# Two layers of attention and feed-forward on one core: new clocks for the program that writes the order of the instructions

## The chip, the cores and the metric

The kernel runs on one core of a Trainium2 chip. The metric is the device time of one execution in microseconds. Three executions of the kernel before took 1618.16, 1618.6 and 1620.25 us (median 1618.6 us); a further one was profiled. The core's engines are TensorE (PE, with its weight loads PEld), VectorE (DVE), ScalarE (ACT), GpSimd (POOL) and SyncE (SP), which issues most DMAs. Each engine works through its own list of instructions in order, and waits on semaphores for what others produce.

## The reference

The input `x` has 2048 rows of 512 (bfloat16). Two equal layers follow each other:

```
x = x + attention(layernorm(x), wqkv, wo)     # 32 heads of 16 columns
x = x + silu(layernorm(x) @ w1) @ w2          # 512 -> 1792 -> 512
```

Attention is `softmax(q k^T / 4) v` over all 2048 keys, so each layer has 32 x 2048 x 2048 exponentials. The result has the shape and type of `x`.

## The kernel before

*Tiles.* Queries are taken in four chunks of 512 rows (`NQC`), heads in eight groups of four (`HB`). One chunk and one group make a segment (`Seg`); there are 74, because some of layer 1's are split into "old" keys (rows 0 to 1535) and "new" keys, so that layer 1 can start before layer 0's last chunk is through its feed-forward. A segment goes over its keys in blocks of 128; a score tile is one key block with two of the four heads, 128 x 1024 numbers in PSUM. There are 2048 score tiles and three PSUM buffers for them (`slot`).

*Scores (L1282).* Two matmuls of 32 rows make a tile. A further row of each head's query carries a bound on the scores, so that no maximum has to be taken. This is the work of `q_pieces`: it loads the raw query `qc` from DRAM (L240), takes its absolute value `qu` (L404), multiplies the keys' maxima `amax` into a small matrix `bm` (L412), forms a product of the two on TensorE (`q_bias`, below "the bias product", tile `q_ps`), and adds it to the query (L421) to make `QT`, the tile that scores read. In the first chunk of layer 0 (segments 0 and 2 to 8) the keys and their maxima are made one segment ahead as well: `k_piece` (matmuls, copy L334, `KT` L321), `amax_piece` (L348) and `amax_all` (L355).

*Exponentials.* Most tiles go to ScalarE (L1503). The others go to VectorE, which writes a bfloat16 bit pattern straight from the scores (L1537); three further terms of the same tile are made by adding constants to the bits, on GpSimd (L1598) or, if the queue of them gets long, on VectorE (L1571). Such a tile has four rows to be multiplied with V instead of one.

*Values (L1358).* Each row is multiplied with V and a column of ones, accumulating in `o_ps`, one bank of PSUM. When a segment's rows are through, `close` copies `o_ps` to `oT` (L1184, L1180 or L1176). A DMA transposes it to `at`; a reciprocal (L513) and a product (L514), both in `heads_norm`, give `attn`.

*The rest.* A chunk's epilogue (`epilogue_pieces`) transposes `attn` by DMA into the buffer `hT`, of which there is one, multiplies with `wo`, and adds to `x`. `ffn_pieces` does the layer norm (L227), the first product with a tanh on ScalarE (L580), L584, and the second product (L593). `next_pieces` does layer 1's norm and V rows (`v_piece`, L379).

*The order.* Nothing is scheduled at run time. The class `Flow` plays the kernel through with a clock for each engine (`self.pe`, `self.act`, `self.dve`, `self.pool`, `self.sp`) and writes each engine's list on the way. `run` lets the engine with the earliest clock take a turn. `pe_turn` chooses between scores of the next tile or two, values whose rows are ready (`fit`), a step of a side piece (`head`: keys, queries, feed-forward), and a fill-in product that nothing reads (`warm`, L1398), which is allowed only while little has run lately. `act_turn` and `dve_turn` and `pool_turn` do the same for theirs. The order is thus as good as the clocks: what each instruction takes, when its result may be read, when a buffer comes free (`slot_free`), and when the port that VectorE and GpSimd share is taken (`lock` by a GpSimd shift, `held_port` by a VectorE operation marked `"l"`).

Before, an operation's end serves both as the time when its engine can go on and, with 50 ns more, as the time when others may read the result:

```
end = self.dve = at + ns
lat = (50, 0, 50)
```

The order does not know when a query tile will be there: `pe_turn` writes the next segment's scores as soon as the step that makes `QT` has been written and a slot is free. The same holds for V rows (`v_made`) and for the buffer `hT`.

*Letters.* Every 16 tiles (`STRETCH`) a letter of `RULES` picks seven settings from `KINDS`: how many spare buffers and how short a queue of shifts are required before VectorE may take a tile, when waiting values go ahead of side work, how fast side work is paid out, when VectorE helps with shifts, and how long it may wait for the port.

Of the kernel before, what the change touches and what calls it, by code (L numbers as in the profile page):

```python
# [20 lines left out]
def kernel(  # L21
# [40 lines left out]
    MM, T_TANH, T_ISSUE, T_LAND, T_POOL = 217, 478, 1450, 2700, 2500  # L62
    M_ISSUE, M_LAND = 400, 2100
# [186 lines left out]
    class Piece:  # L250
        def __init__(self, steps, after=None, lag=0):
# [3 lines left out]
            self.chain = self.key = self.store = None  # L255
# [33 lines left out]
    def ln_pieces(c, cell, after):  # L289
# [11 lines left out]
        return [first, Piece([dve(420, lambda i=i: apply(i), "l") for i in range(4)], free)]  # L301
# [27 lines left out]
    def k_piece(L, c, hb):  # L329
# [10 lines left out]
        ) + [dve(700, out, "c"), dve(302, lambda: k_out(c, hb, cell["st"][:]), "l")])  # L340
# [24 lines left out]
    def amax_all(hb, n, after):  # L365
        return Piece([dve(90, lambda: bm_make(hb, n))], after)
# [8 lines left out]
    def v_piece(tt, L):  # L375
# [10 lines left out]
        return Piece(four(  # L386
            lambda cts: v_mm(tt, cell["ps"][:, :], cts),
            lambda: bank(cell, "v_ps"),
        ) + [dve(700, out, "c")])

# [37 lines left out]
    def bound(seg, cell, after):  # L428

        def bm():  # L430
            cell["bm"] = q_abs_bias(seg.hb)

        return Piece([dve(200, bm, "l")], after)
# [7 lines left out]
    def q_pieces(seg, after, made=None):  # L441
# [23 lines left out]
        if (seg.L, seg.hb) == (0, 0):  # L465
# [3 lines left out]
            ) + [dve(750, c1, "c"), dve(302, c2, "l")])  # L469
        else:  # L470
            first = Piece([("sp", 0, load, "")], made)
            first.chain = cell
            first = Piece([dve(302, c2, "l")], first)
        bm = bound(seg, cell, after)
        last = Piece([pe(MM, d, "o"), dve(700, e, "c")], [first, bm])
        head = first.after if made is not None else []
# [33 lines left out]
    def heads_norm(at_ps, hb, attn):  # L510
        n = at_ps.shape[2]
        rec = bmpool.tile([P, 4, 8, 1], FP32, name="rec", tag="rec")[:, :, 0:n, :]
        nc.vector.reciprocal(rec, at_ps[:, :, :, DH : DH + 1])  # L513
        nc.vector.tensor_tensor(  # L514
            out=attn[:, :, 64 * hb : 64 * hb + DH * n].rearrange("p t (j d) -> p t j d", j=n),
            in0=at_ps[:, :, :, 0:DH],
            in1=rec.to_broadcast([P, 4, n, DH]),
# [5 lines left out]
    def heads_piece(oT, seg, attn):  # L523
# [11 lines left out]
        return Piece([dve(640 if k == 0 else 920, lambda: heads_norm(heads, seg.hb - k, attn))])  # L535
# [118 lines left out]
    def ending(oT, attn, slots, units):  # L654
# [27 lines left out]
        heads_norm(at_ps, hb, attn)  # L682
# [95 lines left out]
    class Seg:  # L778
        def __init__(self, L, c, hb, kind):
            self.L, self.c, self.hb, self.kind = L, c, hb, kind  # L780
            self.kts = {"all": range(TT), "old": range(OLD), "new": range(OLD, TT)}[kind]
            self.QT = None
            self.scaled = kind != "new"
# [156 lines left out]
    class Flow:  # L940

        def __init__(self):
# [29 lines left out]
            self.kept = []  # L972
            self.turned = None
# [9 lines left out]
        def landed(self, at):  # L983
            land = at
            for issue, ns in turns:
                start = max(self.sp, at + 100)
                self.sp = start + issue
                land = max(land, start + ns)
# [66 lines left out]
        def step(self, p, at):  # L1055
# [18 lines left out]
            elif engine == "dve":  # L1074
                if "l" in g:
                    at = max(at, self.lock)
                    self.held_port = at + ns
                end = self.dve = at + ns
                lat = (50, 0, 50)
            else:  # L1080
                self.act = max(at + ns, self.end - 446)
                self.end = max(at + ns + 113, self.end + 491)
# [15 lines left out]
            else:  # L1098
                p.done = True
                if p.chain is not None and p.chain["last"] is p:  # L1100
# [67 lines left out]
        def close(self):  # L1168
# [16 lines left out]
            self.dve = at + 700  # L1185
            self.o_free = self.dve + 50
# [4 lines left out]
            if oT is not None:  # L1191
# [6 lines left out]
                land = self.landed(self.dve)  # L1198
# [16 lines left out]
                if seg.hb == HB - 1:  # L1215
                    ln = {"L": seg.L}
                    new = epilogue_pieces(seg.c, attns[at_], ln)
                    new[0].after = [piece] * (piece is not None)
                    ends[at_] = new[-1:]
                    new += ffn_pieces(seg.c, seg.L == 1, ln, new[-1])  # L1220
                    if seg.L == 0:
# [12 lines left out]
        def due(self):  # L1234

            return self.end + 916 * len(self.exps) - 591 - SWITCH - 60

        def slot_free(self, k):
# [4 lines left out]
            if t.dve:  # L1243
                return max(self.dve, t.at + 475) + 1275
            j = self.exps.index(t)
            return max(self.end + 916 * (j + 1), t.at + 490 + 1017) + 50

        def want_dve(self, t, at, two):
# [9 lines left out]
            return self.dve < at + 475 + LATE  # L1258
# [73 lines left out]
        def fit(self, at):  # L1332

            out = []
            for pr in range(2):
                rows = [
                    r for r in self.lanes[pr]
                    if r[0] <= at and r[1].seg.i == self.open and (r[1].seg.L, r[1].kt) in v_made
                ]
# [69 lines left out]
        def pe_turn(self):  # L1409
# [4 lines left out]
            f = [self.slot_free(k) for k in order]  # L1414
            known = [self.held[k] is None for k in order]
# [70 lines left out]
        def act_turn(self):  # L1486
# [8 lines left out]
            at = max(t, x.at + 490)  # L1495
# [13 lines left out]
            end = max(at + 1017, self.end + 916)  # L1509
# [291 lines left out]
```

## Time and profile before

| | |
|---|---|
| median of three executions | 1618.6 us |
| the profiled execution | 1622.98 us, span 1621.2 us |
| granted TensorE clock, mean | 0.993 |
| ScalarE busy | 1552.8 us (96%) |
| TensorE busy | 1530.3 us (94%) |
| GpSimd busy | 1301.1 us (80%) |
| VectorE busy | 1243.1 us (77%) |
| score tiles on ScalarE (L1503) | 1591, mean 1.19 us of one |
| score tiles on VectorE (L1537) | 457, mean 1.22 us |
| shifts on GpSimd (L1598) / VectorE (L1571) | 1212 / 159 |

In the profile's pages "busy" is the time in which at least one instruction of an engine ran. ScalarE's tiles overlap: one takes 1.19 us from its start to its result, while the ends of two that follow each other lie 0.917 us apart. A group of instructions carries its line, engine, operation, tiles (`out<-in`), sizes, count, busy time and mean, then the idle time in front of it and what ended that. A wait row names who waited for whom, the time in all, how often, and the longest. `v`, `wkq`, `wv_sb` and `idle` in such rows are often no values or weights: their memory is lent to the pool of rows `p` once it is free.

### The profile page before, as it was taken

To read this page: it belongs to the slowest core of one execution; us is meant where nothing else is said; L and a number is where in the kernel's file an instruction comes from. 1 tells how busy PE (TensorE), PEld (TensorE's weight loads), DVE (VectorE), ACT (ScalarE), POOL (GpSimd) and SP (SyncE) were. 2 spreads that over 40 slices of the span, in tenths; PEclk is the share of its full clock that TensorE was granted. 3 is DMA by queue.
4 is the path that set the end of the run, shared out by engine and by line. 5 is a ranking of instruction groups with operands and counts; after the bars stand their busy time and mean duration, and the time that the engine had idled before them with its cause. 6 is when DMAs were issued, how large, how long until landed. Compare 5 with 4: busy or idle time off the path is not lost.

```text
span 1621.2 us, 42218 instructions
## 1 busy us (share of the span) xinstructions
PE 1530.3 (94%) x17118; PEld 482.7 (30%) x17124; DVE 1243.1 (77%) x1561; ACT 1552.8 (96%) x1762; POOL 1301.1 (80%) x1358
## 2 busy tenths in 40 slices
PE   8998989999999999999999999889999999999998
PEld 3222222223322323233322333222322222323233
DVE  7888878786877578776987667787878778778874
ACT  6999989999999999999999998899999999999993
POOL 3989878898899888886667766777989999888990
PEclk9999999999999999999999999999999999999999
DMA  5011011100210011001111011111100110010010
GB/s 195 21 40 29 31 30 27 24 10 8 40 23 14 11 24 43 11 14 24 56 51 41 14 27 33 33 39 43 35 14 11 37 27 11 17 34 21 14 28 14
DMA packets 105747, 49.29 MB, mean 30 GB/s; under 512 B 79024, under 2 KB 105040, under 8 KB 105552
## 3 DMA queue, kind: packets, MB, share of 16 engines
q1 hardware_dynamic: 103536, 45.51, 11.0%
q8 instruction: 134, 2.20, 0.6%
q10 hardware_dynamic: 2016, 1.08, 0.2%
q14 instruction: 61, 0.50, 0.1%
HBM read 17.20 MB, written 11.27 MB: 18 GB/s over the span
## 4 chain that ended last, share of the span: by engine, by line
PE 58%; ACT 17%; DVE 12%; POOL 6%; issue 5%; DMA 1%; ACTq 0%; DVEq 0%; POOLq 0%
PE slot L1282 20%; PE q_ps L1358 19%; ACT p L1503 12%; PE y_ps L312 7%; POOL p L1598 4%; PE h_ps L312 4%; PE k_ps L312 3%; DVE p L1537 3%; ACT v L1503 2%; ACT t_sb L580 2%; POOL v L1598 1%; PE v_ps L312 1%; DVE hT L584 1%; PE q_ps L312 1%; DVE attn L514 1%
## 5 line engine op out<-in xcount | busy, mean ns | idle before, releaser
L1503 ACT ACTIVATE p<-slot 128x1024 bf16<-128x1024 f32 x1206 | 1192.1, 1190 | 24.2 <-PE slot L1282 23.9
L1598 POOL TENSOR_TENSOR p<-p,steps 128x512 int32<-128x512 int32 x658 | 687.3, 1068 | 174.5 <-DVE p L1537 134.1
L1282 PE MATMUL slot<-QT,KT 32*128 32x512 bf16 x4096 | 587.7, 383 | 46.7 <-ACT p L1503 25.6
L1358 PE MATMUL q_ps<-p,v 128*17 128x512 bf16 x4994 | 561.9, 383 | 10.9 <-DVE p L1537 4.0
L1537 DVE TENSOR_SCALAR p<-slot 128x1024 uint16<-128x1024 f32 x331 | 403.8, 1220 | 115.6 <-PE slot L1282 101.8
L1282 PEld LDWEIGHTS <-KT 32*128 32x128 bf16 x4096 | 195.1, 91 | 604.4 <-issue 598.9
L1503 ACT ACTIVATE v<-slot 128x1024 bf16<-128x1024 f32 x268 | 298.3, 1186 | 4.9 <-PE slot L1282 3.6
L1358 PEld LDWEIGHTS <-v 128*17 128x17 bf16 x6838 | 164.1, 88 | 292.5 <-issue 239.4
L1358 PE MATMUL q_ps<-v,v 128*17 128x512 bf16 x1220 | 196.0, 384 | 1.5 <-DVE v L1537 1.1
L1598 POOL TENSOR_TENSOR v<-p,steps 128x512 int32<-128x512 int32 x161 | 172.0, 1074 | 27.7 <-DVE p L1537 18.8
L1598 POOL TENSOR_TENSOR p<-v,steps 128x512 int32<-128x512 int32 x127 | 132.8, 1064 | 16.7 <-DVE v L1537 7.4
L312 PE MATMUL h_ps<-xnT,w_sb 128*32 128x512 bf16 x1568 | 132.4, 384 | 7.1 <-DVE hT L584 6.6
L312 PE MATMUL y_ps<-w_sb,hT 128*32 128x512 bf16 x1568 | 118.0, 382 | 0.1
L1537 DVE TENSOR_SCALAR v<-slot 128x1024 uint16<-128x1024 f32 x72 | 87.9, 1221 | 31.2 <-PE slot L1282 28.7
L584 DVE SCALAR_TENSOR_TENSOR hT<-t_sb,h_ps 128x512 bf16<-128x512 f32 x98 | 66.9, 683 | 46.6 <-ACT t_sb L580 46.4
L312 PE MATMUL k_ps<-xnT,wkq 128*32 128x512 bf16 x960 | 81.0, 389 | 1.5 <-DVE kq L334 1.5
L580 ACT ACTIVATE t_sb<-h_ps 128x512 f32<-128x512 f32 x98 | 76.1, 777 | 0.0
L421 DVE SCALAR_TENSOR_TENSOR QT<-qc,cols,q_ps 128x512 bf16<-128x512 bf16 x74 | 54.9, 742 | 15.6 <-PE q_ps L312 14.5
L1503 ACT ACTIVATE wkq<-slot 128x1024 bf16<-128x1024 f32 x55 | 66.3, 1223 | 0.1
L1598 POOL TENSOR_TENSOR v<-v,steps 128x512 int32<-128x512 int32 x48 | 51.8, 1086 | 10.4 <-DVE v L1537 9.9
L1358 PE MATMUL q_ps<-wkq,v 128*17 128x512 bf16 x328 | 57.7, 381 | 0.0
L312 PEld LDWEIGHTS <-hT 128*32 128x32 bf16 x2016 | 41.0, 95 | 56.2 <-issue 36.6
(166 smaller groups left out, 1493.1 us busy)
## 6 DMA issues: line engine op xcount, KB each, us to landing
qc<-kept_q SPq DMA_DIRECT2D x70, 112.0 KB, 2.0
kept_q<-kq SPq DMA_DIRECT2D x60, 128.0 KB, 1.7
w_sb<-in_B_w_dram SPq DMA_DIRECT2D x2, 1792.0 KB, 12.6
out_dram<-x_sb SPq DMA_DIRECT2D x15, 128.0 KB, 1.7
x_sb<-in_A_x_dram SPq DMA_DIRECT2D x3, 512.0 KB, 7.1
old_q<-QT SPq DMA_DIRECT2D x10, 128.0 KB, 1.7
q_was<-old_q SPq DMA_DIRECT2D x10, 128.0 KB, 2.1
at<-oT SPq DMA_TRANSPOSE x63, 2.3
```

The lines of the kernel that those rows point to most:

```text
L312: nc.tensor.matmul(ps[g, :], lhsT=lhsT[:, g], rhs=rhs, start=start, stop=stop, skip_group_check=True)
L421: nc.vector.scalar_tensor_tensor(out=dst, in0=qc[:], scalar=own, in1=ps, op0=ALU.mult, op1=ALU.add)
L514: nc.vector.tensor_tensor(out=attn[:, :, 64 * hb : 64 * hb + DH * n].rearrange("p t (j d) -> p t j d", j=n), in0=at_ps[:, :, :, 0:DH], in1 ...
L580: nc.scalar.activation(t_sb, ps, ACT.Tanh, scale=0.5)
L584: nc.vector.scalar_tensor_tensor(out=hT[:, ft, :], in0=t_sb, scalar=1.0, in1=ps, op0=ALU.add, op1=ALU.mult)
L1282: nc.tensor.matmul(self.slots[k][:, jj, :], lhsT=KT[32 * j : 32 * j + KR, t.seg.hb, t.kt * P : (t.kt + 1) * P], rhs=t.seg.QT[32 * j : 32 * ...
L1358: nc.tensor.matmul(self.o_ps[32 * j : 32 * j + VW, :], lhsT=vs[seg.L][:, t.kt, 4 * seg.hb + j, :], rhs=buf[:, jj, :], start=not seg.opened ...
L1503: nc.scalar.activation(buf[:].rearrange("p a b -> p (a b)"), self.slots[x.slot][:].rearrange("p a b -> p (a b)"), ACT.Exp, scale=float(SCALE),
L1537: nc.vector.tensor_scalar(out=whole.bitcast(U16), in0=self.slots[x.slot][:].rearrange("p a b -> p (a b)"), scalar1=float(UNIT), scalar2=fl ...
L1598: nc.gpsimd.tensor_tensor(out=b1.bitcast(I32), in0=b0.bitcast(I32), in1=steps32[:, k : k + 1].to_broadcast([P, 512]), op=ALU.add,)
```

## The change

It touches the order's clocks, nothing that is computed:

- *Occupied time and result apart.* A VectorE operation keeps its engine for 96 ns (`PIPE`) less than it takes, and its result may be read by TensorE 99 ns after its end, by VectorE 25 ns after it. ScalarE's and GpSimd's results come 99 and 147 ns after their ends.
- *Ready times.* `q_at` of a segment is when `QT` may be read; `pe_turn` counts a slot for the next tiles as free no earlier than that. `v_at` does the same for V rows in `fit`. `fed` lets a chunk's epilogue start (in SP's queue) only when the feed-forward of the chunk before it has been written to its end.
- *Heads.* `heads_norm` becomes `heads_rec` (reciprocal) and `heads_mul` (product), two steps of one piece, the second marked `"l"`.
- *Costs* of single steps, DMAs and shifts are set anew.
- *Letters.* 128 new letters; `KINDS` stays.

```diff
-    MM, T_TANH, T_ISSUE, T_LAND, T_POOL = 217, 478, 1450, 2700, 2500
-    M_ISSUE, M_LAND = 400, 2100
+    MM, T_TANH, T_ISSUE, T_LAND, T_POOL = 217, 478, 1260, 2500, 2500
+    M_ISSUE, M_LAND = 375, 2050
...
-        return [first, Piece([dve(420, lambda i=i: apply(i), "l") for i in range(4)], free)]
+        return [first, Piece([dve(460, lambda i=i: apply(i), "l") for i in range(4)], free)]
...
-        ) + [dve(700, out, "c"), dve(302, lambda: k_out(c, hb, cell["st"][:]), "l")])
+        ) + [dve(700, out, "c"), dve(424, lambda: k_out(c, hb, cell["st"][:]), "l")])
...
-        return Piece([dve(90, lambda: bm_make(hb, n))], after)
+        return Piece([dve(160, lambda: bm_make(hb, n))], after)
...
+        p.value = (L, tt)
+        return p
...
-        return Piece([dve(200, bm, "l")], after)
+        return Piece([dve(289, bm, "l")], after)
...
-            first = Piece([dve(302, c2, "l")], first)
+            first = Piece([dve(291, c2, "l")], first)
         bm = bound(seg, cell, after)
         last = Piece([pe(MM, d, "o"), dve(700, e, "c")], [first, bm])
+        last.query = seg
...
-    def heads_norm(at_ps, hb, attn):
-        n = at_ps.shape[2]
-        rec = bmpool.tile([P, 4, 8, 1], FP32, name="rec", tag="rec")[:, :, 0:n, :]
+    def heads_rec(at_ps):
+        m, n = at_ps.shape[1:3]
+        rec = bmpool.tile([P, 4, 8, 1], FP32, name="rec", tag="rec")[:, 0:m, 0:n, :]
         nc.vector.reciprocal(rec, at_ps[:, :, :, DH : DH + 1])
+        return rec
+
+    def heads_mul(at_ps, rec, hb, attn):
+        m, n = at_ps.shape[1:3]
         nc.vector.tensor_tensor(
...
-        return Piece([dve(640 if k == 0 else 920, lambda: heads_norm(heads, seg.hb - k, attn))])
+        cell = {}
...
+        return Piece([dve(252 if k == 0 else 354, first), dve(536 if k == 0 else 757, second, "l")])
...
-                start = max(self.sp, at + 100)
+                start = max(self.sp, at + 20)
...
                 if "l" in g:
                     at = max(at, self.lock)
-                    self.held_port = at + ns
-                end = self.dve = at + ns
-                lat = (50, 0, 50)
+                    self.held_port = at + ns - PIPE + 20
+                end = at + ns
+                self.dve = end - PIPE
+                lat = (99, 25, 50)
             else:
-                self.act = max(at + ns, self.end - 446)
-                self.end = max(at + ns + 113, self.end + 491)
+                self.act = max(at + ns, self.end - 396)
+                self.end = max(at + ns + 200, self.end + 491)
...
                 p.done = True
+                if p.query is not None:
+                    p.query.q_at = end + 99
+                if p.value is not None:
+                    self.v_at[p.value] = end + 99
...
-            self.dve = at + 700
-            self.o_free = self.dve + 50
+            self.dve = at + 604
+            self.o_free = at + 799
...
-                    new[0].after = [piece] * (piece is not None)
+                    new[0].after = [p for p in (piece, self.fed) if p is not None]
                     ends[at_] = new[-1:]
                     new += ffn_pieces(seg.c, seg.L == 1, ln, new[-1])
+                    self.fed = new[-1]
...
-            return self.end + 916 * len(self.exps) - 591 - SWITCH - 60
+            return self.end + 917 * len(self.exps) - 565 - SWITCH - 60
...
             if t.dve:
-                return max(self.dve, t.at + 475) + 1275
+                return max(self.dve, t.at + S_DVE) + T_PASS + 99
             j = self.exps.index(t)
-            return max(self.end + 916 * (j + 1), t.at + 490 + 1017) + 50
+            return max(self.end + 917 * (j + 1), t.at + S_ACT + 1052) + 99
...
+                    and self.v_at.get((r[1].seg.L, r[1].kt), 0) <= at
...
             f = [self.slot_free(k) for k in order]
+            for k, x in enumerate(tiles[self.n : self.n + 2]):
+                f[k] = max(f[k], x[0].q_at)
...
-            end = max(at + 1017, self.end + 916)
+            end = max(at + 1052, self.end + 917)
...
-            self.free[x.slot] = end + 50
+            self.free[x.slot] = end + 99
             self.held[x.slot] = None
-            self.row(x, end + 50, buf, 0)
+            self.row(x, end + 99, buf, 0)
...
-                self.dve = at + T_PASS
-                self.free[x.slot] = self.dve + 50
+                self.dve = at + T_PASS - PIPE
+                self.free[x.slot] = at + T_PASS + 99
...
-                self.dve = t + T_BITS
-                self.held_port = self.dve
-                self.row(x, self.dve + 50, x.bufs[k][1], k)
+                self.dve = t + T_BITS - PIPE
+                self.held_port = self.dve + 20
+                self.row(x, t + T_BITS + 99, x.bufs[k][1], k)
...
-            self.pool = self.lock = t + T_SHIFT
-            self.row(x, self.pool + 80, x.bufs[k][1], k)
+            self.pool = t + T_SHIFT
+            self.lock = self.pool - 40
+            self.row(x, self.pool + 147, x.bufs[k][1], k)
...
-    SWITCH, T_PASS, T_BITS, T_SHIFT = 100, 1225, 430, 1000
+    SWITCH, T_PASS, T_BITS, T_SHIFT = 100, 1234, 427, 997
+    PIPE, S_DVE, S_ACT = 96, 450, 430
...
-        "mmmmllllllllllllCCCCCCCCCCCCCCCCmmmmmmmmmmmmBBBBvvvvdddddddddddd"
-        "aaaaaaaakkkkkkkknnnnnnnnddddddddwwwwwwwwwwwwwwwwhhhhyyyynnnnaaaa"
+        "mmmmddddddddddddlllllllldddddddduuuuuuuujjjjuuuullllllllllllllll"
+        "jjjjjjjjeeeeeeeewwwwwwwwooooooooAAAAAAAAyyyyyyyysssslllloooooooo"
```

## The prediction, made before the changed kernel was run

> **What bounds the kernel now.** I read the busy shares first, then ScalarE's waits, then ScalarE in the stretches where it waits, then the chain and TensorE's waits there, last VectorE.
>
> ```profile
> PE 1530.3 (94%) x17118; PEld 482.7 (30%) x17124; DVE 1243.1 (77%) x1561; ACT 1552.8 (96%) x1762; POOL 1301.1 (80%) x1358
> ACT p L1503 <- PE slot L1282: 23.9, 34, 2.4
> ACT v L1503 <- PE slot L1282: 3.6, 4, 1.5
> ACT idle L1503 <- PE slot L1282: 1.1, 2, 0.6
> ```
>
> ACT is the bound. From its first score tile (32 us) to its last (1578 us) it idles 30.3 us in all (these three rows, and 1.0 + 0.5 + 0.2 in smaller ones), nearly always for TensorE's scores. 99% of its pairs of exponentials end between 912 and 925 ns after one another. So whatever the change does between 32 and 1578 us comes through those 30.3 us or through the number of tiles on ACT.
>
> ```profile
> 78.50:82.50 4.00, 3.48 (x5) 1.00 0.00 0
> 149.50:157.50 8.00, 6.52 (x8) 0.79 0.00 0
> ...
> 798.00:802.00 4.00, 2.28 (x3) 1.00 0.44 126
> 817.50:825.50 8.00, 6.10 (x7) 0.79 0.40 99
> ...
> 997.50:1001.50 4.00, 1.91 (x3) 1.00 0.26 66
> 1005.00:1009.00 4.00, 2.69 (x4) 1.00 0.09 29
> sum 60.00, ACT 48.35; mean ACT 3.72
> ```
>
> These are ACT's busy times (then the granted clock) in 13 short stretches, each where the scores of a new segment start: 60.00 - 48.35 = 11.65 us of the 30.3 lie in 4% of the time. From 240 to 700 us, the same view gives ACT 459.87 of 460 us busy. The chain says what happens there:
>
> ```profile
> 996.75 0.65 PE q_ps L1398 x12
> 997.40 0.28 PE q_ps L1358 x2
> 997.74 0.57 issue
> 998.31 0.75 DVE QT L421
> 999.10 0.45 PE slot L1282 x4
> ...
> PE slot L1282 <- DVE QT L421: 9.1, 13, 0.9
> PE q_ps L1358 <- DVE p L1537: 4.0, 7, 1.9
> PE slot L1282 <- DVE p L1537: 3.9, 6, 1.5
> ```
>
> TensorE ran fill-in products (L1398), then stood until VectorE had written the query tile `QT` (L421), and only then wrote the segment's first scores. This happens 13 times. The other waits are for VectorE rows that come late; the worst is before 218.6 us:
>
> ```profile
> 212.41 1.27 DVE L321 TENSOR_SCALAR KT<-kq,cols 128x512 bf16<-128x512 bf16 x1
> 213.61 0.34 DVE L513 RECIPROCAL rec<-at 128x32 f32<-128x32 bf16 x1
> 213.98 1.15 DVE L514 TENSOR_TENSOR attn<-at,rec 128x512 bf16<-128x512 bf16 x1
> 215.05 1.26 DVE L1571 TENSOR_SCALAR p<-p 128x1024 int16<-128x1024 int16 x1
> ```
>
> L321 and L1571 took 1.27 and 1.26 us here; their minima in the trace are 404 and 408 ns. They start while POOL's shifts (L1598) run and wait for them.
>
> **The change, part by part.** The counts here are those of the two programs' instruction orders.
>
> *Work.* Exponentials on ACT go from 1591 to 1590: -0.92 us at 917 ns. Tiles that VectorE takes instead (L1537) go from 457 to 458. Scores, keys, values, feed-forward keep their counts. TensorE's value groups with one matmul pair alone fall from 727 to 706 and fill-in products from 560 to 463 single matmuls, by about 217 ns a group (the spacing of groups in the trace): TensorE has 94% busy and is waited for only at the places above, so this counts as nothing; its cover is ACT's backlog of three score tiles. VectorE's share of shifts (L1571) goes from 159 to 185, POOL's from 1212 to 1189. 26 more at L1571's mean of 754 ns are 19.6 us on VectorE; 25 of them lie in tiles 256 to 768 (225 to 601 us); from 240 to 700 us VectorE was busy 348 of 460 us and ACT idled 0.13. Cost taken: 0. If that cover is gone, the nearest row is the 4.0 + 3.9 us above, doubled.
>
> *Query clocks (`q_at`, the q steps' costs, the result's 99 ns, the letters).* In the order of before I counted TensorE's steps between a segment's bias product and its first scores. Segments 2 to 8 have 0, 0, 1, 0, 2, 2, 0 steps, segments 32, 33, 34 have 1, 0, 2, segments 42, 43, 44 have 0, 3, 6 (three of these fill-ins in each of the last two): the 13 waits. What must pass in between is bias product, QT (740 ns) and two hand-overs, 1.2 us start to start (79.93: 1223 ns; 103.75: 1242), five to six steps. In the new order the same segments have 7, 3, 7, 9, 7, 9, 4; 47, 16, 11; 23, 13, 17, and all but segment 3 have 1 to 17 score tiles of the old segment among them, so ACT has work meanwhile. Fill-ins written because the next query did not exist: 20 groups before, 2 after. Segments 3, 50 and 55 now have no score tile in between and 3 or 4 steps. So -11.65 us, and back 3 x 11.65/13 = +2.7 us: -8.95. Bounds: all 11.65 gone, or nothing, if the bias product itself is then late (rival 2).
>
> *Late rows.* The rest of ACT's idle time, 30.3 - 11.65 = 18.65 us. The costs of what shares the port with POOL come nearer the trace (KT 302 to 424, bm 200 to 289, trace minima 404 and 267), the heads' product is put behind POOL's shift (`l`), separate from its reciprocal. This removes no instruction. It may place rows better: from -18.65 to, with as much again, +18.65. I take 0, since the contended part (L1571's mean over all forms less its minimum, 754 - 408 ns, 159 times, 55 us of VectorE) is left and there are more of them.
>
> *V rows, feed-forward tile, SP.* No wait of TensorE for a copied V row stands among its rows above 0.6 us, so `v_at` is worth 0 (bounds -0.6 to 0.6). `fed` writes the epilogue's four transposes into SP's queue only after the previous feed-forward; behind them stand query loads, whose lateness cost VectorE 2.1 us in two waits. 0, bounds -2.1 to +2.1 (a transpose that is issued later can be missed too: `y_ps` waited 2.5 us for `hT`). Split heads: the same two instructions. Opening (0 to 32) and ending (1578 to 1621): same instructions but one tail step, 0.2 us.
>
> Sum: -0.92 - 8.95 = -9.9 us. The profiled execution took 1622.98 us (span 1621.2), 0.27% over the median of 1618.6; it should become 1613.1, and the median 1608.7.
>
> **Clock.** Before has six stretches of 3.4 us at half clock inside the run (152, 220, 234, 821, 1039, 1050 us), each behind a TensorE gap of 0.9 to 2.3 us; those at 152 and 821 lie in the 13 windows and are in the 11.65. The Trainium skill (TensorE: Matmul & The Clock Gate, Part 1) says that the clock is granted by how busy the array was in windows of 3.4 us. By that rule 97 fewer fill-ins speak against the change, and the sum would be that of rival 4 in place of 1608.7; the trace agrees on the length and on gaps coming first, and no run yet shows whether fewer fill-ins alone do it. The Trainium skill (SBUF — State Buffer, section SBUF: two separate sides) says that VectorE and GpSimd hold their common port exclusively for a whole instruction; the 1.26 us beside 0.41 agree, and by it 26 more VectorE shifts speak against the change, towards the sum of rival 3.
>
> **Rivals.**
> 1. *Late rows shrink too* (1602). The better port costs and fewer half-clock stretches take a further third, 6.2 us, of the 18.65. For: 220 and 234 us start with VectorE late by unmodelled waits. Against: VectorE's load grows. Chance 0.17.
> 2. *The wait moves up one step* (1613). The bias product gets late: it needs `bm` and `qu`, which wait for POOL (412: 267 to 1133 ns; 404: 275 to 1151). For: three bias products already stood 0.6 to 0.8 us (102.5, 149.5, 837.5). Half of the 8.95 stays: -5.4. Chance 0.15.
> 3. *VectorE's rows become the bound* (1624): slower. Place: 80 to 240 us, where VectorE is busy 133.6 of 160 us and must make keys, maxima, bias and query of the next segment in each 24 us. One such event cost ACT 2.6 us (215 to 224 us: 6.39 of 9 busy). Six more, 15.6 us, give +5.7; it decides from (9.9 + 3.2)/2.6 = 5 events. Against: that part's counts of L1571 and L1537 hardly change. Chance 0.11.
> 4. *The clock drops oftener* (1618.8): without fill-ins, half-clock stretches double; six more at the 1.7 us of ACT that those at 152 and 821 cost (1.48 and 1.90, from the windows) are +10.1 us and eat the gain. Chance 0.06.
> 5. *Nothing of it happens*, queries late as before: 1617.7. Against: the counted steps. Chance 0.03.
>
> **How the numbers follow.** The forecast has 0.48, and a change within 0.2% (3.2 us) is about what a measurement here can't tell from none. Faster: 0.48 + 0.17 + 0.14 of rival 2 and 0.01 of rival 5 = 0.80; same: 0.01 + 0.04 + 0.02 = 0.07; slower: 0.11 + 0.02 of rival 4 = 0.13. Range 1599 to 1619: below, rival 1 with half of the late rows gone; above, rivals 4 and 5; outside remain rival 3 and a tail of rival 1, under 0.2.
>
> **What would show it.** PE's wait for `QT` falls from 9.1 us and 13 times to 3 us or less; ACT's waits for `slot` fall from 28.6 us to about 20; at the starts of segments 32, 33, 42, 43, 44 ACT runs through; L1503's count is 1590; L1571 has 185 at 700 to 800 ns. I am wrong if ACT's idle time has moved to 80 to 240 us behind `p` of VectorE, or if the half-clock stretches are more than six.

## The result and the profile after

The changed kernel takes 1597.83 us (1597.37 to 1598.11), the kernel before 1618.71 beside it: a ratio of 0.9869, 95% interval 0.9852 to 0.9886. That is 20.9 us faster; forecast were 9.9 us, and 1597.8 lies under the range (1599 to 1619). The direction was right; the forecast gain was half of the measured one.

Part of the gain is TensorE's clock. Beside the experiments, 42 further executions of the kernel before are on record. The lower the granted clock of one, the longer it took: 1614.4 us at 0.999, 1624.6 us at 0.989, about 0.9 us for each thousandth. A straight line through them gives 1614.5 us at a clock of 1.000 (an estimate). By this estimate some 4 of the 20.9 us are stretches at half clock that no longer come, and some 17 us remain between two kernels at full clock.

The profiled execution took 1597.37 us with a span of 1595.6, 25.6 us under the profiled one of before; that one was 4.3 us over its kernel's median, and at its clock of 0.993 the same line stands some 6 us above its end at 1.000. Busy shares of the changed kernel, then all of ScalarE's waits between its first and last score tile:

```profile
PE 1523.0 (95%) x17024; PEld 482.7 (30%) x17030; DVE 1253.2 (79%) x1588; ACT 1549.9 (97%) x1761; POOL 1283.5 (80%) x1335
ACT p L1530 <- PE slot L1306: 4.6, 9, 1.1
ACT wv_sb L1530 <- PE slot L1306: 1.1, 1, 1.1
ACT idle L1530 <- PE slot L1306: 0.3, 1, 0.3
ACT wkq L1530 <- PE slot L1306: 0.2, 1, 0.2
ACT p L1530 <- PE q_ps L1383: 0.2, 1, 0.2
ACT v L1530 <- PE slot L1306: 0.2, 1, 0.2
```

ScalarE idles 6.6 us in these rows where it idled 30.3, so 23.7 us of the 25.6 are in them. One tile less is 0.9. The starts and ends of its tiles give the rest: from the first tile's start to the last one's end the run got 26.6 us shorter, 2.0 more than idle time and the tile explain. The rest stands at the gaps themselves. Where one tile follows another with a gap, their ends lie 917 ns, the gap and another 107 ns apart, since the second can no longer overlap with the first. There are 49 such gaps in the trace before and 28 after: 21 x 107 ns = 2.2 us. The ending, from ScalarE's last tile to the end, grew by 1.1 us (42.7 to 43.8).

The same segment starts as before, ScalarE's busy time and the granted clock (2, 5, 32, 33, 43, 44), and the start of segment 50:

```profile
76.50:80.50 4.00, 4.00 (x6) 1.00 0.00 0
146.00:154.00 8.00, 8.00 (x10) 1.00 0.12 33
785.50:789.50 4.00, 4.00 (x5) 1.00 0.10 34
803.00:811.00 8.00, 7.98 (x10) 1.00 0.30 68
980.50:984.50 4.00, 3.99 (x6) 1.00 0.18 49
987.50:991.50 4.00, 4.00 (x5) 1.00 0.10 33
1059.00:1063.00 4.00, 2.94 (x4) 1.00 0.18 47
```

Over all 13 starts that were late before, ScalarE is busy 59.77 of 60 us (48.35 before). Only segment 50, one of the three that the forecast named as still short, loses 1.06 us. TensorE's waits:

```profile
PE slot L1306 <- DVE p L1564: 3.9, 11, 0.5
PE q_ps L1383 <- DVE oT L1207: 1.2, 5, 0.4
...
PE q_ps L1383 <- DVE p L1564: 0.7, 1, 0.7
PE slot L1306 <- DVE QT L423: 0.5, 1, 0.5
```

The kernel before had, beside the rows shown with the prediction:

```profile
PE q_ps L1358 <- DVE oT L1180: 3.7, 5, 1.3
```

TensorE's wait for `QT` fell from 9.1 us in 13 places to 0.5 us in one. But its waits for late rows of VectorE fell as well: `q_ps` for `p` from 4.0 to 0.7 and `q_ps` for `oT` from 3.7 to 1.2. The wait for a score tile's buffer (`slot`) that VectorE still reads is 3.9 us as before, but its longest is 0.5 us instead of 1.5, and the longest wait for a row in the trace before, 1.9 us, has no counterpart. The forecast had let those stand. The six half-clock stretches inside the run are gone; the granted clock is 1.00 throughout.

### The profile page after: what moved, and what is told of

Read it like the earlier page. It is cut to its first block, busy times and chain, and to the rows that moved or that the text cites. A ratio compares the mean times of both kernels' runs of the same rounds, so it can differ in the third digit from the quotient of the medians.

```text
span 1595.6 us, 41986 instructions
## 1 busy us (share of the span) xinstructions
PE 1523.0 (95%) x17024; PEld 482.7 (30%) x17030; DVE 1253.2 (79%) x1588; ACT 1549.9 (97%) x1761; POOL 1283.5 (80%) x1335
## 4 chain that ended last, share of the span: by engine, by line
PE 51%; ACT 25%; DVE 13%; issue 6%; POOL 3%; DMA 1%; ACTq 0%; DVEq 0%; POOLq 0%
PE slot L1306 18%; ACT p L1530 17%; PE q_ps L1383 14%; PE y_ps L312 7%; PE h_ps L312 4%; ACT v L1530 3%; DVE p L1564 3%; PE k_ps L312 3%; ACT t_sb L595 2%; POOL p L1625 2%; DVE hT L599 1%; PE v_ps L312 1%; ACT wkq L1530 1%; DVE v L1564 1%; DVE p L1598 1%
## 5 line engine op out<-in xcount | busy, mean ns | idle before, releaser
L1530 ACT ACTIVATE p<-slot 128x1024 bf16<-128x1024 f32 x1164 | 1163.5, 1204 | 5.4 <-PE slot L1306 4.6
L1530 ACT ACTIVATE v<-slot 128x1024 bf16<-128x1024 f32 x280 | 316.9, 1203 | 0.3 <-PE slot L1306 0.2
L1625 POOL TENSOR_TENSOR v<-p,steps 128x512 int32<-128x512 int32 x143 | 152.8, 1075 | 25.2 <-DVE p L1564 22.7
L1625 POOL TENSOR_TENSOR p<-v,steps 128x512 int32<-128x512 int32 x145 | 154.4, 1083 | 12.3 <-DVE v L1564 11.0
L1564 DVE TENSOR_SCALAR v<-slot 128x1024 uint16<-128x1024 f32 x82 | 100.0, 1219 | 25.7 <-PE slot L1306 24.4
L1530 ACT ACTIVATE wkq<-slot 128x1024 bf16<-128x1024 f32 x80 | 93.5, 1212 | 0.2 <-PE slot L1306 0.2
L1598 DVE TENSOR_SCALAR p<-p 128x1024 int16<-128x1024 int16 x98 | 69.6, 713 | 1.0
L1625 POOL TENSOR_TENSOR v<-v,steps 128x512 int32<-128x512 int32 x52 | 56.0, 1081 | 8.8 <-DVE v L1564 8.8
## 6 DMA issues: line engine op xcount, KB each, us to landing
w_sb<-in_B_w_dram SPq DMA_DIRECT2D x2, 1792.0 KB, 13.3
```

What stands on the lines that cost most here:

```text
L1530: nc.scalar.activation(buf[:].rearrange("p a b -> p (a b)"), self.slots[x.slot][:].rearrange("p a b -> p (a b)"), ACT.Exp, scale=float(SCALE),
L1564: nc.vector.tensor_scalar(out=whole.bitcast(U16), in0=self.slots[x.slot][:].rearrange("p a b -> p (a b)"), scalar1=float(UNIT), scalar2=fl ...
L1598: nc.vector.tensor_scalar(out=x.bufs[k][1][:].rearrange("p a b -> p (a b)").bitcast(I16), in0=whole.bitcast(I16), scalar1=SHIFTS[k], scala ...
L1625: nc.gpsimd.tensor_tensor(out=b1.bitcast(I32), in0=b0.bitcast(I32), in1=steps32[:, k : k + 1].to_broadcast([P, 512]), op=ALU.add,)
```

## Experiments

The program that writes the order keeps count of what its own clocks lose on ScalarE (`self.lost`). Beside that *planned* loss stands the *idle* time of ScalarE in the trace, from its first score tile to its last (by the starts and ends of its instructions; 0.4 us less than the wait rows add up to, before and after alike). The difference is what the clocks *missed*; clocks that miss little are called honest here. This is the measure in which the variants can be compared, because each edit changes the whole order, and letters that suit one set of clocks plan long stalls with another. All times are medians, beside 1617.7 to 1620.7 us of the kernel before in the same jobs.

| kernel | tiles on ScalarE | planned us | idle us | missed us | time us |
|---|---|---|---|---|---|
| before | 1591 | 6.3 | 29.9 | 23.6 | 1618.7 |
| before, new letters | 1598 | 31.0 | 47.1 | 16.1 | 1647.5 |
| before, letter m | 1595 | 23.8 | 44.5 | 20.7 | 1642.6 |
| before, heads split | 1599 | 33.9 | 53.3 | 19.4 | 1655.7 |
| before, `q_at` | 1591 | 40.2 | 50.4 | 10.2 | 1643.0 |
| before, `q_at` and heads split | 1594 | 49.7 | 54.3 | 4.6 | 1649.5 |
| changed, old costs | 1607 | 30.8 | 29.2 | -1.6 | 1637.2 |
| changed without `q_at` | 1588 | 28.0 | 51.2 | 23.1 | 1641.6 |
| changed, heads joined, unmarked | 1587 | 17.0 | 34.9 | 17.9 | 1632.9 |
| changed, heads split, unmarked | 1586 | 27.4 | 39.4 | 12.0 | 1630.8 |
| changed, heads joined, marked | 1595 | 18.0 | 19.1 | 1.1 | 1616.9 |
| changed without `fed` | 1591 | 2.3 | 8.2 | 5.8 | 1601.3 |
| changed, old letters | 1586 | 32.4 | 33.9 | 1.5 | 1627.5 |
| changed, letter m | 1584 | 35.9 | 39.0 | 3.1 | 1627.4 |
| changed, letters by earliest end of ScalarE | 1585 | 0.8 | 10.7 | 10.0 | 1610.3 |
| changed, letters by earliest end of TensorE | 1589 | 1.5 | 8.9 | 7.4 | 1601.2 |
| changed | 1590 | 2.3 | 6.2 | 3.8 | 1597.8 |

How far can the last column but one be trusted? The changed kernel profiled a second time (`changed_again`) idles 5.5 us instead of 6.2. Another order moves it more: with one and the same clocks, five sets of letters miss between 1.5 and 10.0 us on the new clocks, three sets 16.1 to 23.6 on the old. So a difference of less than some 8 us between two rows can be the luck of the order.

`v_at` was not run: without its line each engine's list is the same, instruction for instruction, so it is worth nothing here.

### Letters and clocks, crossed

```diff
 # letters_only: the kernel before with RULES of the changed kernel
 # letters_old: the changed kernel with RULES of the kernel before
 # before_all_m, after_all_m: either kernel with
+    RULES = "m" * 128
```

> The kernel before with the new letters alone; all clocks as before. In this order 14 segments start with no score tile of the old segment behind their bias product (13 in the kernel before, 3 in the changed one) and ScalarE gets 1598 tiles (1591 before, 1590 changed). Theory 'late queries by the clocks': ACT idles as in the kernel before, about 14 x 0.9 + 18.65 = 31 us, and 7 more tiles cost 6.4 us: 1625 us. Rival 'the letters carry the gain': 1607 us or less.

> The changed kernel with the old letters; all clocks new. 12 segments start without a score tile behind their bias product, ScalarE has 1586 tiles. If a late start costs 0.9 us and the rest of the gain comes from clocks that are nearer the trace: 1597.8 + 9 x 0.9 - 4 x 0.92 = 1602 us. If late rows, too, come back without letters that fit: 1597.8 + 8 + 15 - 4 = 1617 us. If the letters do nothing: 1594 us.

> The kernel before with one letter (m) for all tiles, so that no letters are fitted to its clocks. 13 late starts, 1595 tiles on ScalarE. Theory 'late queries': 1618.7 + 3.7 = 1622 us. If the old letters were fitted to hide much of what the clocks miss: 1630 us or more.

> The changed kernel with the letter m for all tiles. 11 late starts, 1584 tiles on ScalarE. If the clocks alone carry the gain: some 20 us under the kernel before with letter m, so about 1602 us. If the gain needs letters that fit: within 5 us of the kernel before with letter m less 11 tiles x 0.92 us.

Measured: 1647.48, 1627.53, 1642.59 and 1627.40 us. New letters on old clocks are slower than the kernel before (ratio 1.0183, 1.0159 to 1.0207), old letters on new clocks too (1.0054, 1.0032 to 1.0076). Neither half of the change gains alone.

By the theory of late queries I had expected 1625, 1602, 1622 and 1602 us, 21 to 26 too little, because a price of 0.9 us for each late start leaves out what mattered: with letters that don't suit them, either clocks plan stalls of up to 15 us where a query cannot be made in time (the longest at segment 42, tile 1264, in three of the four), and these happen. What does tell the theories apart is the last column but one. With new clocks and these three sets of letters 1.5 to 3.8 us are missed; with old clocks 16 to 24. On one and the same letter the new clocks are 15.2 us faster, 10.1 of it because they give ScalarE 11 tiles less (0.917 us each) and 5.5 from idle time. The run with letter m thus lies between its two expectations, 5.1 us under that of "needs letters that fit" and 4.8 us short of the 20 us of "the clocks alone", and does not decide between them. The clocks bring honesty, and the letters then choose an order that is short by honest clocks: 2.3 us planned, 6.2 idle. The old letters had chosen one that was short by clocks that missed 23.6.

### The ready time of queries

```diff
 # no_q_at: the changed kernel without
-            for k, x in enumerate(tiles[self.n : self.n + 2]):
-                f[k] = max(f[k], x[0].q_at)
 # q_at_only: the kernel before with these lines and the two that set q_at
```

> The changed kernel without the two lines that hold a score slot until the query tile can be read. What the order's own clocks lose on ScalarE (planned) and what the trace shows (idle) are compared: kernel before 6.3 planned, 30.3 idle, so 24 us missed; changed kernel 2.3 and 6.6, 4 missed. This variant plans 28.0 us and has 1588 tiles on ScalarE, 12 late query starts. If the ready time of queries makes the clocks honest: 4 + 12 x 0.7 = 12 us missed, 1597.8 - 1.8 + (28 + 12 - 6.6) = 1629 us. If it does nothing for honesty: 4 us missed, 1621 us.

> The kernel before with the ready time of queries alone (old costs, old letters). Its clocks plan 40.2 us, 1591 tiles on ScalarE. If late queries were 9 of the 24 us missed before: 15 missed, 1647 us. If they were all of it: 4 missed, 1636 us. If they were none: 24 missed, 1656 us.

Measured: 1641.56 and 1642.95 us. Without `q_at` the changed kernel misses 23.1 us, as much as the kernel before; TensorE's wait for `QT` is back:

```profile
PE slot L1306 <- DVE QT L423: 7.0, 10, 1.0
```

With it alone, the kernel before misses 10.2 us instead of 23.6. So `q_at` is worth 13 us of missed time on the old clocks (the forecast had 11.65 us of late starts) and 19 on the new, both more than the letters alone move it. In `no_q_at` the expectation was short by 12 us. It may be that all that stands behind a late query on TensorE is late by the clocks as well, but this is not shown. The clock has a part in it: that trace has four half-clock stretches, 20.5 us in all, and 13.4 us of ScalarE's idle time, some of it planned, lies from 3 us before to 4 us behind each.

### Costs and result times

```diff
 # costs_old: the kernel before with q_at, fed, the split heads and the new letters;
 # costs, latencies, PIPE as before:
+            for k, x in enumerate(tiles[self.n : self.n + 2]):
+                f[k] = max(f[k], x[0].q_at)
...
+                    new[0].after = [p for p in (piece, self.fed) if p is not None]
...
+        return Piece([dve(252 if k == 0 else 354, first), dve(536 if k == 0 else 757, second, "l")])
```

> The changed kernel's ready times (queries, feed-forward), split heads and new letters on the kernel before's costs and latencies. It plans 30.8 us and gives ScalarE 1607 tiles. If costs and result times carry the honesty: 18 us missed, 1597.8 + 17 x 0.92 + (30.8 + 18 - 6.6) = 1656 us. If the ready times carry it: 4 missed, 1642 us.

Measured: 1637.22 us, and -1.6 us missed. The ready times and the split heads make the clocks honest; of new costs this program has only those of the heads' two steps, 788 and 1111 ns together instead of 640 and 920, and of new latencies only the 99 ns behind `QT`. The theory that all the other costs and result times carry it fell. What they do is another thing: with `PIPE` the order sees 96 ns more room behind each VectorE operation, and the changed kernel gives VectorE 17 tiles more than this one with the same letters. (Played through with `PIPE` at 0 and nothing else altered, without a run, the changed program gives ScalarE 1608 tiles, about as many as here.) How much of the gain they would keep with letters that suit each was not tried, so their share stays open.

### The heads' step

```diff
 # heads_joined: the changed kernel with one step again
+        return Piece([dve(640 if k == 0 else 920, both)])
 # heads_unmarked: two steps, the product without "l"
+        return Piece([dve(252 if k == 0 else 354, first), dve(536 if k == 0 else 757, second)])
 # heads_whole: one step at the full cost, marked
+        return Piece([dve(692 if k == 0 else 1015, both, "l")])
 # heads_only: the kernel before with the changed kernel's two steps
 # q_at_heads: the same, and q_at
```

> The changed kernel with reciprocal and product of the heads as one step again, not marked for the port. It plans 17.0 us, 1587 tiles on ScalarE. If the split only reorders: 4 us missed, 1597.8 - 2.8 + (17 + 4 - 6.6) = 1609 us. If the unmarked product is what the clocks missed (its port wait is some 0.4 us in 42 places): 12 us missed, 1617 us.

> The kernel before with the ready time of queries and the heads' product split off and marked for the port; old costs, old letters, no wait for the feed-forward's tile. Plan 49.7 us, 1594 tiles. With the ready time of queries alone 10 us were missed. If the split takes the rest: 2 us missed, 1597.8 + 3.7 + (49.7 + 2 - 6.2) = 1647 us. If it takes nothing: 1655 us.

> The kernel before with the heads' product split off and marked, nothing else. Plan 33.9 us, 1599 tiles. If the split alone removes 10 of the 24 us missed: 14 missed, 1597.8 + 8.3 + (33.9 + 14 - 6.2) = 1648 us. If it removes nothing: 24 missed, 1658 us.

> The changed kernel with the heads' product as a step of its own but not marked for the port. Plan 27.4 us of ScalarE lost, 1586 tiles. Joined and unmarked, 18 us were missed by the clocks; split and marked 4. If the mark (the clocks' knowledge that the product waits for POOL's shift) is what counts: 12 us or more missed, 1597.8 - 3.7 + (27.4 + 12 - 6.2) = 1627 us or more. If the split is: 4 missed, 1619 us.

> The changed kernel with reciprocal and product as one step of 692 or 1015 ns, marked for the port as a whole. Plan 18.0 us, 1595 tiles. If the mark and the full cost are what counts: 4 us missed or fewer, 1597.8 + 4.6 + (18 + 4 - 6.2) = 1618 us. If the split is: 12 or more missed, 1626 us or more.

Measured: 1632.86, 1649.47, 1655.67, 1630.80 and 1616.91 us. Joined and unmarked, the changed kernel misses 17.9 us; split but unmarked 12.0; joined but marked 1.1. So it is the mark, with the full cost, that counts. Cost and mark were not separated cleanly: the step from 17.9 to 12.0 adds the split and the cost, the one from 12.0 to 3.8 the mark, and each is no more than letters can move; only the two together, 17.9 against 1.1, are clear of that.

That the product waits for GpSimd's shifts stands in the trace. Of the 21 products with 256 numbers a row (of each partition) in the kernel before, 19 start while a shift (L1598) runs, and each of them ends 280 to 283 ns after that shift's end, be the rest of the shift 0.2 or 1.0 us. The two others take 424 ns. `heads_whole` is within 0.3% of the kernel before (0.9980, 0.9965 to 0.9995): its letters plan 18.0 of the 19.1 us that ScalarE idles; its clocks are as honest as the changed kernel's. The split in itself gave nothing that the mark doesn't. On old clocks the split and marked product takes 4.2 us off what is missed (23.6 to 19.4), and 5.6 once `q_at` is there (10.2 to 4.6). That would mean that the two causes add up, but neither difference is larger than what letters can move.

VectorE's rows of the kernel before, the reciprocal and the product, then those of `heads_joined` (mean of one behind the comma):

```profile
L513 DVE RECIPROCAL rec<-at 128x16 f32<-128x16 bf16 (+1 forms) x42 | 12.4, 295 | 4.1 <-DMA at<-oT 4.0
L514 DVE TENSOR_TENSOR attn<-at,rec 128x256 bf16<-128x256 bf16 (+1 forms) x42 | 39.6, 943 | 1.4
```

```profile
L521 DVE TENSOR_TENSOR attn<-at,rec 128x256 bf16<-128x256 bf16 (+1 forms) x42 | 43.5, 1036 | 1.4
L516 DVE RECIPROCAL rec<-at 128x16 f32<-128x16 bf16 (+1 forms) x42 | 12.3, 293 | 4.6 <-DMA at<-oT 4.6
```

The step takes 295 + 943 = 1238 ns on average. The clocks of before allowed 640 or 920, 780 on average: each of the 42 steps left VectorE up to 0.46 us later than the order knew, 19 us in all, and the rows behind it late. TensorE's waits for `p` in `heads_joined` show it beside the changed kernel's 3.9 and 0.7 and the 4.0 and 1.3 of `heads_whole`:

```profile
PE slot L1310 <- DVE p L1568: 7.1, 17, 1.1
...
PE q_ps L1387 <- DVE p L1568: 3.2, 6, 1.1
```

### The feed-forward's tile

```diff
 # no_fed: the changed kernel with
-                    new[0].after = [p for p in (piece, self.fed) if p is not None]
+                    new[0].after = [piece] * (piece is not None)
```

> The changed kernel with the epilogue free to start before the feed-forward of the chunk before it has been written. Its clocks plan 2.3 us of ScalarE lost, as the changed kernel's do; 1591 tiles. If that ready time is worth nothing: 4 us missed, 1598.7 us. If transposes that wait in SP's queue for the one hT buffer hold up query loads and heads behind them: 8 us or more missed, 1603 us or more.

Measured: 1601.31 us, 3.5 more than the changed kernel, with 5.8 us missed (3.8) and one tile more. TensorE waits for `QT` no longer than in the changed kernel (0.2 us). One half-clock stretch came in at 729 us, where ScalarE is busy 8.71 of 10 us. So `fed` is worth some 3.5 us in this order, hardly more than medians of the kernel before differ from job to job (3.0 us), and not through late queries; whether it kept that one stretch away or the new order merely happened to, this run cannot say.

### The fill-in products

```diff
 # no_fill: the changed kernel, in warm()
-            for j in range(1 if narrowly else 4):
+            for j in range(0):
```

> The changed kernel without the 463 fill-in products in the main part; the order of everything else is the same, and the output too, since nothing reads them. If TensorE's clock needs them: half-clock stretches come back, six or more, at 1.7 us each, 1608 us or more. If the work itself keeps the clock: no half-clock stretch or one, 1598 us.

Measured: 1605.60 us, 7.8 us more than the changed kernel. The edit takes out 458 of the 463 products; five belong to the ending. Six half-clock stretches are back in the main part, 34 us in all, at 222, 649, 673, 1031, 1096 and 1144 us. Windows around three of them in `no_fill`, then in the changed kernel (TensorE, weight loads, VectorE, ScalarE, GpSimd, granted clock):

```profile
215.00:225.00 10.00, 8.55 (x72) 2.21 (x68) 6.91 (x10) 9.60 (x11) 8.73 (x9) 0.85 0.10 25
640.00:660.00 20.00, 17.54 (x170) 4.49 (x166) 12.30 (x14) 17.02 (x21) 13.18 (x14) 0.83 0.04 8
1030.00:1050.00 20.00, 18.72 (x152) 4.08 (x150) 14.01 (x20) 17.59 (x20) 15.12 (x15) 0.74 0.09 26
```

```profile
215.00:225.00 10.00, 9.14 (x96) 2.55 (x92) 7.83 (x11) 9.86 (x12) 8.17 (x8) 1.00 0.11 26
640.00:660.00 20.00, 18.21 (x212) 5.76 (x208) 14.82 (x17) 20.00 (x25) 17.06 (x17) 1.00 0.05 13
1030.00:1050.00 20.00, 19.29 (x190) 5.87 (x188) 17.26 (x23) 20.00 (x23) 18.27 (x18) 1.00 0.07 21
```

In the two longer windows ScalarE runs 20.00 of 20 us with the fill-ins, 17.0 and 17.6 without. So the clock does need them, at work that keeps TensorE 94% busy without them and 95% with them. Not all of the 7.8 us is theirs: the first score tile starts 1.2 us later than in the changed kernel, behind a half-clock stretch at 10 us that three runs with the fill-ins (`letters_old`, `heads_unmarked`, `heads_whole`) have as well. The changed kernel has 97 fewer of them than the kernel before and still no half-clock stretch. From one group of TensorE's to the next it has at most 1.4 us (2.3 before); but it has steps of 0.9 to 1.4 us as well, as stood before some of the half-clock stretches in the kernel before and in `no_fill`, so which gap tips the clock is not settled here. By the Trainium skill (TensorE: Matmul & The Clock Gate, Part 1), how busy the array was decides on the clock in windows of 3.4 us. These traces agree: the stretches last 3.4 us or a multiple, and products that nothing reads are enough to keep them away.

### Letters chosen by the new clocks

```diff
 # letters_new: the changed kernel, RULES from a search for the earliest end of ScalarE's clock
+        "mmmmddddddddddddlllllllldddddddduuuuuuuujjjjuuuullllllllllllllll"
+        "jjjjjjjjeeeepeeewwmcwwttooovqqoobbbbbbbbyyyyyyyyssssllllCCCCCCCC"
 # letters_end: the same, for TensorE's clock and the side work left over at the end
+        "mmmmddddddddddddlllllllldddddddduuuuuuuujjjjuuuullllllllllllllll"
+        "jjjjjjjjeueeeeeewwhhwwwwooooooooAAAAAAAtyyyyyyyymmmmllllccccccss"
```

> The changed kernel with letters chosen so that its own clocks end earliest: they plan 0.8 us of ScalarE lost (2.3 in the changed kernel) and 1585 tiles on it (1590). If the clocks are honest (4 us missed, as in the changed kernel): 1597.8 - 5 x 0.92 - 1.5 = 1591.7 us. If the small misses of the changed kernel were found by fitting letters to the chip, not to the clocks: 10 us or more missed, 1598 us or more.

> As the letters run before it, but with letters for which the end of TensorE's clock and the side work left over together come earliest. Planned against the changed kernel: 3.2 us less, 1589 tiles on ScalarE (1590), 1.5 us of ScalarE lost (2.3). If the clocks are honest to a microsecond or two: 1594.6 us, under both kernels. If what they miss differs from order to order by more than that: anywhere from 1593 to 1602 us.

> The changed kernel once more beside it, on the same chip: 1597.8 us by every theory.

Measured: 1610.26, 1601.20 and 1598.19 us. Neither set of letters beats the changed kernel. `letters_new` had a target that did not count side work: 11.6 us of it was left undone when the last tile came, and the ending took 55.1 us instead of 43.8. It also missed 10.0 us, 5.5 us of it around one half-clock stretch of 13.7 us:

```profile
1440.00:1480.00 40.00, 37.30 (x350) 8.94 (x342) 32.40 (x41) 34.51 (x38) 33.71 (x39) 0.83 0.11 26
```

`letters_end` planned 3.2 us less than the changed kernel and came out 3.0 us slower than it in the same job. It idles 8.9 us, 7.4 of them missed, and has two half-clock stretches (217 and 1292 us) where the changed kernel has none. So the new clocks are honest to 2 to 10 us. Part of what they miss stands around half-clock stretches: 5.5 of 10.0 us in `letters_new`, 2.6 of 7.4 in `letters_end` (from 3 us before to 4 us behind each), none of the changed kernel's 3.8. The program counts how much TensorE ran lately, to place its fill-ins, but none of its clocks slows down with the array's. A plan that is 3 us shorter is not yet a faster run.

## Why the prediction was right and wrong

*Bound.* Right: ScalarE's idle time and tile count carry the result (23.7 + 0.9 of 25.6 us in the profiled executions). I left out that every gap also costs the overlap of two tiles, 107 ns each time, 2.2 us for the 21 gaps that went.

*Late queries, -8.95.* Right in place and nearly in size: the 13 stretches went from 11.65 to 0.23 us. Of the three segments that I charged 2.7 us as still short, one lost 1.06 us, so the term measured -10.4. That the ready time of queries carries it is confirmed in both directions (`no_q_at`, `q_at_only`). The steps that I had counted between bias product and scores are another matter: `q_at` alone doesn't put them there. In `letters_old` 12 segments still start without a score tile in between; the clocks then plan the wait (32.4 us planned, 1.5 missed) instead of running into it. Only with letters that suit the new clocks are the steps there as well.

*Late rows, 0.* This is the step that failed, and with it "Split heads: the same two instructions". The 18.65 us that I held fixed became 5.3 (6.6 less the 0.23 and 1.06 us counted above). I priced the part by the instructions it issues, which are the same, not by what the order learns from it, namely that the heads' product waits for the port. The profile had the figure: 295 + 943 ns in the trace against 640 or 920 in the code, 42 times, 19 us of VectorE. I had even shown the event, L514 at 1.15 us before the gap at 218.6 us, and named L321 and L1571 as its cause, whose wait for the port the old clocks knew (both are given to `lock`, one by its mark, one in its own code). The product was the one port user there that they didn't know. `heads_joined` and `heads_whole` (17.9 and 1.1 us missed) show it. Not all of the 13.3 us is shown to be this. In the profiled execution of before, 7.7 us of the 18.65 lie from 3 us before to 4 us behind the four half-clock stretches outside the 13 starts, and none of these came in the changed kernel. Whether rows that come in time kept them away, or the new order happened to, no run separates.

*VectorE's load, 0.* Right but for 1.3 us: there are 185 shifts of L1571's kind (mean 737 ns), and from 240 to 700 us, where most of the further ones lie, ScalarE idled 1.4 of 460 us instead of 0.1.

*`v_at`, 0.* Right, since the lists are the same without it. *`fed`, 0 within 2.1.* The run without it was 3.5 us slower, a little outside.

*Rivals.* Rival 1 (late rows shrink too) is what happened, at twice its price: some seven tenths of the rows' idle time went, not a third. I had given it 0.17 and put "VectorE late by unmodelled waits" into it without asking which operation was unmodelled. Rival 2 did not happen (TensorE waited 0.7 us in all for `qu` and `bm`), and neither did rival 3: from 80 to 240 us VectorE is busier than before (140.4 of 160 us), and ScalarE still runs 159.6. Rival 4 was wrong about this kernel and right about its mechanism: the fill-ins keep the clock, but those that are left are enough. Rival 5 fell with the counted steps.

*Letters.* They stand in no term of the sum. Either set alone, on the other clocks, is slower than the kernel before; I had only counted what the two together do, which was enough for the direction.

## What to carry to other kernels

Where a program plays engines through to write their order, compare each cost and each ready time in it with the trace's row, contended mean and all; steps times the difference says how late the engine runs behind the plan. Leave out of it what the program waits for by another clock: here `bm` (706 ns against 200, 74 times, 37 us) stood ahead of the heads' 19 us by this product, but it is marked for the port, so the order had its wait in the plan. What was missed came from one unmarked step and one unknown ready time. Planned loss beside measured loss is the figure to judge such a model by, since every edit reshuffles the order and its time alone says little. Settings fitted to a wrong model have to be fitted again once it is mended, or the mending looks like a loss.

## What the runs showed of the hardware

- 458 single matmuls of TensorE's 17,000 whose results nothing reads keep six half-clock stretches (34 us in all) away. Without them the kernel takes 7.8 us of 1598 longer, some 1.2 us of it for another reason. TensorE's busy time (94% without them, 95% with them) does not tell the two apart.
- A VectorE product (L514, 256 numbers a row) that starts while a GpSimd shift runs ends 280 to 283 ns after the shift does, however much of the shift was left; alone it takes 424 ns. VectorE's own shifts (L1571) do the same, nearly all 281 to 288 ns behind GpSimd's, against 408 to 449 ns alone.
- A gap between two of ScalarE's score tiles costs 107 ns beyond its own length.
